# Sums of a weight block in one go, a product behind the operand splits, and two transfers asked for one pair sooner

## The chip, the cores and the metric

The kernel runs on one core of one Trainium2 chip. The metric is the device time of the whole program in microseconds (us). A core has one engine for matrix products (TensorE, PE in the profile, with its weight loads as PEld), three for elementwise work (VectorE = DVE, ScalarE = ACT, GpSimd = POOL), and a queue, SyncE (SP), which here issues all transfers between memory and the core. Each engine works through its own instructions in order and waits where an operand or a buffer is not ready.

## The reference

Two branches read the same input x of 2048 rows and 640 columns (written A_x and B_x in the inputs; x stands for A_x).

```python
xn = _layernorm(x)                                    # first branch: on the normalised rows
q, k, v = (xn @ wqkv) split into 32 heads of 20
logits  = q . k[pos - 2*w] * 20**-0.5,  w = 0..7      # a local window of 8 rows, 2 apart
attn    = softmax(logits, masked where pos - 2*w < 0)
s       = (sum over w of attn * v[pos - 2*w]) @ wo

g = x @ w_gate                                        # second branch: 640 -> 1536
u = x @ w_up
out = x + s * silu((g * u) @ w_down)                  # 1536 -> 640
```

So there are four large products (wqkv, gate and up, wo, w_down), and between the first and the third the attention, which is elementwise work on 32 heads.

## The kernel before, in words

All products are taken to the precision of float32 as three products of parts: each operand is split into a high part (`hi`, rounded for TensorE) and the remainder (`lo`). `split` (L104, L105) does it: ACT writes hi, then GpSimd writes lo. A product is hi·hi, hi·lo, lo·hi (`ALL3`).

The order of all instructions is written out by hand: each engine works in the order in which the program issues them.

1. Loading, layer norm and transpositions, to about 100 us.
2. The product with wqkv in 12 units of 8 tiles (`qkv`, L395); ACT copies each result (L401) and SP stores it (L403). Beside it runs the attention, a generator that `advance` steps on as time passes: DVE multiplies and reduces (L470, L480, L444), GpSimd adds up the output o (L447, with every second addition on DVE in the last unit), and `store_o` (L522) writes o to memory (`o_scr`). The attention is behind the products and goes on beside stage 3, until about 485 us.
3. Gate and up, one column block f = 2 to 11 after another, from about 276 to 541 us. x is taken in four chunks of 512 rows, 0 to 3. For chunks 0 and 1, `group(f)` forms seven products (L1197) of sums of weight blocks and sums of x (Strassen's scheme in Winograd's form), in the order j = 0, 5, 2, 1, 4, 3, 6. For chunks 2 and 3 the products are plain: `gate(f, 2)`, `gate(f, 3)`, `up(f, 2)`, `up(f, 3)`, each of 15 matmuls (L114).
4. The product of o with wo, by pairs of tiles p = 0 to 4 (`pair_product`, L935), and three tiles by themselves, until about 611 us; beside it the sums and splits of w_down.
5. The last products with w_down (L802) and the output, to the end.

In stage 3, the sums of the next block's weights (`w_add`, L1149) are GpSimd's: S1, S2, S3, d5, S4, written to a tile `wraw`. `w_split` splits them in two groups, S (S1 to S3) and R (S4 and d5); the gate's and up's own columns are G and U. The seven products go into three banks: A, B and C. Of chunk 1's result, `gate_b` (L1174, DVE) completes the gate and `up_b` the up half: an addition (L1177) and the product of both (L1178) on GpSimd, and then the store of h (`store_h`, L1161). Of chunk 0's, `gate_a` (L1182) and `up_a` (L1185) are DVE's. What stands in the list `unfinished` is issued by the next `finish_piece`: `up_a` in `gate(f, 2)` that follows the group, behind its 15 matmuls and the copy of their result by ACT (L1226). Between `group(f)` and `gate(f, 2)` stands `next_sums(f + 1)`. So GpSimd has, per block: S1, S2, an addition of o, S3, d5, an addition of o, the addition of `up_b`, its product, S4, the lo parts of S and R, an addition of o. ACT has the hi parts of S and R and then the copy of `gate(f, 2)`.

The first block of these, f = 2, has its sums and the splits of S and G made during stage 2: `first_parts` is a list of seven steps, of which `paced` takes 0.42 at each of the 8 tiles of a unit; what is left at the end is made at once (`step(100)`).

In stage 4, `load_pair(p)` asks for the two tiles of o of pair p in four transfers (`load_o`, L619), and `turn_pair(p)` transposes them on DVE (L625) and forms sums (L887 to L890). `hi_pair` (L910, ACT) and `lo_pair` (L914, DVE) split them. `pair_product` copies or adds a result (L938, L941, L944, L946, L949) and stores it (L947, L950). The raw tiles of pairs 1, 3 and 4 share the two buffers of the tag "t". `out_proj` does the single tiles (ACT copies L651 and L664, DVE L653), and the w_down sums are DVE's (L705, L708, L712, L715).

Of the kernel before, what the change touches and what calls it, by code (L numbers as in the profile page):

```python
# [51 lines left out]
def kernel(  # L52
# [23 lines left out]
    def st(shape, tag, bufs, dt=F32):  # L76
        cnt[0] += 1
        return sb.tile(shape, dt, tag=tag, bufs=bufs, name=f"{tag}_{cnt[0]}")
# [39 lines left out]
    def slot(shape, dt=F32R):  # L118
        return st(shape, "s", SLOTS, dt)
# [221 lines left out]
    UN = [(g, r) for g in range(len(GROUPS)) for r in range(DIL)]  # L341
# [238 lines left out]
    unfinished = []  # L580
# [34 lines left out]
    def load_o(s, n, t):  # L615


        for b in range(NQ):
            nc.sync.dma_start(t[b * QB:(b + 1) * QB].rearrange("i n (q c) -> i (n q) c", c=QC),  # L619
                              o_scr[s // NE, b, s % NE:s % NE + n].rearrange("n (q i) c -> i (n q) c", i=QB))  # L620
        for i in range(n):
            o_t[s + i] = t[:, i]
# [249 lines left out]
    def load_pair(p):  # L872
        t = slot([P, 2, D], F32) if p == 2 else st([P, 2 if p else 6, D], "t" if p else "kv", 2)
        if not p:
            wo_sum.append(t[:, 2:].rearrange("p a (b c) -> p (a b) c", c=HALF))
            t = t[:, :2]
        load_o(2 * p, 2, t)
        t = t.rearrange("p a c -> p (a c)")
        pair_raw[p] = t[:, :3 * KS * P].rearrange("p (a c) -> p a c", c=P)
# [43 lines left out]
    def pair_product(p, j):  # L923
        place = "ACACABA"[j]
        new = j in (0, 1, 5)
        if new:
            bank[p, place] = pt([P, HALF], {"A": "q", "B": "g", "C": "u"}[place], {"A": 3, "B": 2, "C": 2}[place])
        b = bank[p, place]
        runs = [(pair_in(p, H_IN[j], k, i), w_part(W_IN[j], k, l)) for i, l in ALL3 for k in range(KS)]
        if j in FIFTH:  # L930
            name, c = FIFTH[j]
            runs += [(pair_in(p, name, 0, i), wo_t["W0-W1"][:, l] if c is None else wo_s[KD - 1][l][:, c:c + HALF])
                     for i, l in ALL3]
        for r, (y, w) in enumerate(runs):
            nc.tensor.matmul(b, y, w, start=new and r == 0, stop=r == len(runs) - 1, skip_group_check=True)  # L935
        kept, (ya, yb) = pair_k[0], y_t.setdefault((p, "y"), [None, None])
        if j < 3:
            nc.scalar.activation(kept[:, j], b, AF.Copy)  # L938
        elif j == 3:
            ya = y_t[p, "y"][0] = st([P, D], "gh", 5)  # L940
            nc.vector.tensor_add(ya[:, HALF:], kept[:, 2], b)  # L941
        elif j == 4:
            yb = y_t[p, "y"][1] = st([P, D], "gh", 5)
            nc.vector.tensor_add(yb[:, HALF:], kept[:, 1], b)  # L944
        elif j == 5:
            nc.vector.tensor_add(ya[:, :HALF], kept[:, 0], b)  # L946
            nc.sync.dma_start(s_scr[2 * p], ya)  # L947
        else:
            nc.scalar.activation(yb[:, :HALF], b, AF.Copy)  # L949
            nc.sync.dma_start(s_scr[2 * p + 1], yb)  # L950
# [189 lines left out]
    def w_add(f, *names):  # L1140

        if f not in w_sum:
            w_sum[f] = st([P, 9, P], "wraw", 2)
        r, t = wf_raw[f], w_sum[f]
        v = {"A11": r[:, 0:2, 0], "A12": r[:, 2:4, 0], "A21": r[:, 0:2, 1], "A22": r[:, 2:4, 1], "g5": r[:, 4, 0],
             "u5": r[:, 4, 1], "S1": t[:, 0:2], "S2": t[:, 2:4], "S3": t[:, 4:6], "S4": t[:, 6:8], "d5": t[:, 8]}
        for name in names:
            a, b = W_SUM[name]
            nc.gpsimd.tensor_tensor(v[name], v[a], v[b], op=ALU.add if name == "S1" else ALU.subtract)  # L1149
# [14 lines left out]
    def group(f):  # L1164

        b = {"A": pt([P, CH], "g", 2), "C": pt([P, CH], "u", 2), "B": q_one}
        kept, later = {}, []

        def hold(j):
            kept[j] = st([P, CH], "gh", 5)  # L1170
            nc.scalar.activation(kept[j], b["ACACABA"[j]], AF.Copy)  # L1171

        def gate_b():
            nc.vector.tensor_add(kept[2], kept[2], b["C"])  # L1174

        def up_b():
            nc.gpsimd.tensor_add(kept[1], kept[1], kept[4])  # L1177
            nc.gpsimd.tensor_mul(kept[2], kept[2], kept[1])  # L1178
            store_h(f, 1, kept[2])

        def gate_a():
            nc.vector.tensor_add(kept[0], kept[0], b["B"])  # L1182

        def up_a():
            nc.vector.tensor_mul(kept[0], kept[0], b["A"])  # L1185
            store_h(f, 0, kept[0])

        w_split(f, "U")
        wf_raw.pop(f)
        for n, j in enumerate((0, 5, 2, 1, 4, 3, 6)):  # L1190
            y = b["ACACABA"[j]]
            runs = [(w_unit(H_IN[j], k)[i], x_in(W_IN[j], l, k)) for i, l in ALL3 for k in range(2)]
            if j in FIVE:
                name, ch = FIVE[j]
                runs += [(w_unit(name)[i], xT[ch][l][:, KD - 1, :]) for i, l in ALL3]
            for r, (w, x) in enumerate(runs):
                nc.tensor.matmul(y, w, x, start=j in (0, 1, 5) and r == 0, stop=r == len(runs) - 1,  # L1197
                                 skip_group_check=True)
            if j in (0, 1, 2, 4):
                hold(j)  # L1200
            finish_piece()
            for act in later:
                act()
            later = {5: [gate_a], 3: [gate_b, up_b]}.get(j, [])
            if j == 6:
                unfinished.append(up_a)
            if f < f1 and n in (3, 4):
                w_add(f + 1, *(("S1", "S2"), ("S3", "d5"))[n - 3])
            if n in beside:
                beside[n]()  # L1210
            advance(PACE * len(runs) * 0.184)
# [34 lines left out]
        advance(PACE * 2.8)  # L1246

    def next_sums(f):
        w_add(f, "S4")
        w_split(f, "S", "R")  # L1250
        w_sum.pop(f)
        if f < f1:
            load_wf(f + 1)
# [11 lines left out]
    paced = 0.0  # L1265
    for u in range(2, len(UN)):
        begin_unit(u)
        g, r = UN[u]
        for i in range(NE):
            if g + 1 < len(GROUPS) and (r, i) == (0, 1):  # L1270
                load_wq(g + 1, ((0, 3), (3, 5)))
            elif g + 1 < len(GROUPS) and r and i < KD:
                split_wq(g + 1, nc.gpsimd, (i, i + 1))
            if u == len(UN) - 3 and i == 6:
                load_wf(2)
            qkv(u, i)
            if i == 1:
                finish_piece()
            advance(PACE * GROUPS[g] * 0.38)
            paced += 0.42  # L1280
            while paced >= 1:
                paced -= 1
                step()
        if u == len(UN) - 3:
            steps.append(first_parts())
        elif u == len(UN) - 2:
            for k in range(2):
                last_difference(k)
# [71 lines left out]
    def wd_splits():  # L1360
        while to_split:
            k, part = to_split.pop(0)
            split_wd(k, part)
            if part and k + 2 < KH:
                load_wd(k + 2)

    pair_product(0, 0)
    for p in range(SP // 2):
        more = p + 1 < SP // 2
        if not more:  # L1370
            y1 = turn_o(SP)
        if p < 3:
            wd_sums()
        pair_product(p, 1)
        if more:
            hi_pair(p + 1, 0)
            lo_pair(p + 1, 0)
            if p == 3:
                wd_sums()
        else:  # L1380
            split_o(SP, y1)
        pair_product(p, 2)
        if not more:
            wd_splits()
            wd_sums()
        elif p < 3:
            hi_pair(p + 1, 2)
        pair_product(p, 3)
        if more:
            if p == 3:  # L1390
                hi_pair(p + 1, 2)
            lo_pair(p + 1, 2)
            hi_pair(p + 1, 1)
        pair_product(p, 4)
        wd_splits()
        if more:
            lo_pair(p + 1, 1)
        pair_product(p, 5)
        if p == 0:
            load_pair(3)  # L1400
        elif p == 1:
            load_pair(4)
            turn_pair(3)
        elif p == 2:
            load_o(SP, 3, st([P, 3, D], "t", 2))
            turn_pair(4)
        else:
            if p == 3:
                load_o(SP + 3, 3, st([P, 3, D], "t", 2))
            wd_sums()  # L1410
        if more:
            pair_product(p + 1, 0)
        else:
            out_proj(SP, 0)
            wd_splits()
        pair_product(p, 6)
# [25 lines left out]
    for m in range(n_prod):  # L1442
        n, j = divmod(m, 7)
# [65 lines left out]
```

## Time and profile before

| what | value |
|---|---|
| time, median of 3 runs | 769.35 us (766.48 to 770.05) |
| the profiled execution's own time | 765.59 us |
| its span | 763.8 us |
| mean granted TensorE clock | 0.997 |
| PE busy | 748.3 us |
| DVE busy | 601.5 us |
| GpSimd busy | 422.7 us |
| ACT busy | 276.0 us |

How to read it: the span is the stretch between the first and the last instruction of one profiled execution, and the time is a little longer. Busy times are sums over instructions. A line of a timeline gives the start in us from the span's beginning, the duration, the engine, the line of the kernel, the operation with its output and input tiles and their shapes, and in brackets how long the engine was idle before it and what released it. A group of waits gives the engine, the tile and the line that waited, what it waited for, the total in us, the number of times and the longest. The ends of matmuls are modelled, and a run of matmuls is shown as one row.

### The profile page before, as it was taken

How to read it: one execution, taken by the hardware profiler on the slowest of the kernel's cores; microseconds unless marked ns; L12 is line 12 of the kernel's file. 1: busy time of each engine (PE TensorE's matmuls, PEld its weight loads, DVE VectorE, ACT ScalarE, POOL GpSimd, SP SyncE). 2: the span in 40 equal slices, each digit the busy share in tenths (PEclk: the TensorE clock that was granted, in tenths of full speed). 3: DMA queues.
4: the chain of work that ended last, by engine and by line, in shares of the span. 5: the costliest groups of instructions: out<-in, count | busy, mean ns of one | idle time of the engine just before them, and what ended most of it. 6: DMA issues, size and time to landing. Idle time of an engine off the chain costs nothing. (4 is left out here: it accounts for less than half of the span.)

```text
span 763.8 us, 11642 instructions
## 1 busy us (share of the span) xinstructions
PE 748.3 (98%) x4342; PEld 688.4 (90%) x4342; DVE 601.5 (79%) x753; ACT 276.0 (36%) x534; POOL 422.7 (55%) x342
## 2 busy tenths in 40 slices
PE   8999999999999999999999999999999999999997
PEld 6989899999999988888888787788999999999997
DVE  7899995997796896989696967244888697777775
ACT  4334213233332232222222222234465564444442
POOL 5100256988966969799787987664648810000000
PEclk9999999999999999999999999999999999999999
DMA  9463537678458454464535331544487565555534
GB/s 326 142 189 101 159 105 204 209 198 217 157 161 240 134 177 127 116 185 125 145 105 148 90 87 29 170 109 105 132 224 212 186 251 186 187 187 186 186 104 139
DMA packets 101975, 123.02 MB, mean 161 GB/s; under 512 B 24376, under 2 KB 75956, under 8 KB 101918
## 3 DMA queue, kind: packets, MB, share of 16 engines
q1 hardware_dynamic: 101918, 122.28, 52.6%
q8 instruction: 34, 0.56, 0.3%
q14 instruction: 23, 0.19, 0.1%
HBM read 78.73 MB, written 42.81 MB: 159 GB/s over the span
## 5 line engine op out<-in xcount | busy, mean ns | idle before, releaser
L447 POOL TENSOR_TENSOR o<-o,t 128x800 f32<-128x800 f32 (+1 forms) x81 | 164.3, 2029 | 56.3 <-DVE o L444 45.8
L105 POOL TENSOR_TENSOR s<-wraw,s 128x768 fp32r<-128x768 f32 (+5 forms) x72 | 89.1, 1253 | 82.8 <-ACT s L104 72.1
L114 PE MATMUL g<-xc,s 128*128 128x512 f32 (+1 forms) x435 | 101.2, 387 | 4.0 <-DVE gh L1185 2.9
L470 DVE TENSOR_TENSOR t<-q,kv 128x1600 f32<-128x1600 f32 (+1 forms) x48 | 92.5, 1927 | 12.2 <-DMA kv<-qkv_scr 8.3
L114 PEld LDWEIGHTS g<-xc,s 128*128 128x128 f32 x435 | 80.6, 191 | 20.7 <-DVE gh L1185 3.3
L114 PE MATMUL u<-xc,s 128*128 128x512 f32 (+1 forms) x435 | 99.1, 383 | 0.0
L114 PEld LDWEIGHTS u<-xc,s 128*128 128x128 f32 x435 | 79.7, 188 | 15.7
L480 DVE TENSOR_REDUCE lg<-t 128x80 f32<-128x1600 f32 (+1 forms) x48 | 92.3, 1923 | 0.1
L444 DVE TENSOR_TENSOR t<-e,kv 128x800 f32<-128x800 f32 (+1 forms) x84 | 87.1, 1036 | 5.4 <-POOL o L447 5.3
L395 PE MATMUL q<-s,xc 128*128 128x300 f32 (+1 forms) x540 | 84.5, 307 | 1.4 <-DVE rstd L249 0.7
L395 PEld LDWEIGHTS q<-s,xc 128*128 128x128 f32 x540 | 79.4, 188 | 2.6 <-DVE rstd L249 1.0
L104 ACT ACTIVATE s<-wraw 128x640 fp32r<-128x640 f32 (+5 forms) x73 | 43.0, 601 | 93.4 <-POOL wraw L1149 55.5
L395 PE MATMUL g<-s,xc 128*128 128x300 f32 (+1 forms) x420 | 65.8, 308 | 0.0
L395 PE MATMUL u<-s,xc 128*128 128x300 f32 (+1 forms) x420 | 65.4, 307 | 0.0
L395 PEld LDWEIGHTS g<-s,xc 128*128 128x128 f32 x420 | 62.4, 188 | 0.0
L395 PEld LDWEIGHTS u<-s,xc 128*128 128x128 f32 x420 | 62.1, 188 | 0.0
L802 PE MATMUL q<-xc,s 128*128 128x320 f32 x270 | 42.0, 309 | 0.0
L802 PEld LDWEIGHTS q<-xc,s 128*128 128x128 f32 x270 | 40.2, 188 | 0.0
L1197 PE MATMUL g<-xc,s 128*128 128x512 f32 x150 | 37.5, 390 | 1.0 <-POOL s L105 1.0
L1238 DVE TENSOR_TENSOR gh<-u,gh 128x512 f32<-128x512 f32 x19 | 13.0, 686 | 30.7 <-PE u L114 30.7
L1171 ACT ACTIVATE gh<-g 128x512 f32<-128x512 f32 x30 | 18.0, 599 | 52.5 <-PE g L1197 51.7
L765 DVE TENSOR_TENSOR s<-s,s 128x768 fp32r<-128x768 f32 x29 | 27.8, 958 | 8.9 <-ACT s L761 8.8
(304 smaller groups left out, 1339.1 us busy)
## 6 DMA issues: line engine op xcount, KB each, us to landing
h_scr<-gh SPq DMA_DIRECT2D x48, 256.0 KB, 2.4
qkv_scr<-s SPq DMA_DIRECT2D x28, 300.0 KB, 3.7
wraw<-in_wgu SPq DMA_DIRECT2D x11, 640.0 KB, 4.4
t<-h_scr SPq DMA_DIRECT2D x8, 768.0 KB, 7.3
qkv_scr<-s SPq DMA_DIRECT2D x16, 360.0 KB, 3.1
kv<-qkv_scr SPq DMA_DIRECT2D x14, 400.0 KB, 5.1
s_scr<-gh SPq DMA_DIRECT2D x16, 320.0 KB, 3.5
gh<-s_scr SPq DMA_DIRECT2D x16, 320.0 KB, 4.0
```

The source lines that it names most:

```text
L104: nc.scalar.activation(hi, raw, AF.Copy)
L105: eng.tensor_sub(lo, raw, hi.bitcast(F32))
L114: nc.tensor.matmul(acc, a, b, start=first and n == 0, stop=last and n == len(runs) - 1)
L395: nc.tensor.matmul(p, xT[(r * NE + i) // TPC][a][:, k, t0:t0 + P], wq[g][b][k], start=n == 0, stop=n == len(runs) - 1, skip_group_check=ac ...
L444: nc.vector.tensor_mul(t.rearrange("p (n d) -> p n d", d=DH), e[:, :, w].unsqueeze(2).to_broadcast([P, NE * nh, DH]), v)
L447: return NE * c * cost, lambda: eng.tensor_add(y, y, t)
L470: nc.vector.tensor_mul(t, q, k)
L480: nc.vector.tensor_reduce(out=lg[:, :, j:j + 2].rearrange("p n a -> p a n"), in_=t.rearrange("p a (n d) -> p a n d", d=DH), op=ALU.add, ax ...
L765: nc.vector.tensor_sub(hT[m][:, 1], h_raw[n][name], hT[m][:, 0].bitcast(F32))
L802: nc.tensor.matmul(p, y[:, i, k], wd_t[name][k][:, l], start=new and r == 0, stop=r == len(runs) - 1, skip_group_check=True)
L1171: nc.scalar.activation(kept[j], b["ACACABA"[j]], AF.Copy)
L1197: nc.tensor.matmul(y, w, x, start=j in (0, 1, 5) and r == 0, stop=r == len(runs) - 1, skip_group_check=True)
```

## The change

There are four edits.

1. `up_b` keeps only the addition. The product and its store become a function `h_b`, which is put in `unfinished` ahead of `up_a`: it is issued behind the splits of S and R of the next block and behind the matmuls and the copy of `gate(f, 2)`.
2. S4 is made in `group` together with S3 and d5, no longer in `next_sums`. GpSimd's order per block becomes S1, S2, an addition of o, S3, d5, S4, an addition of o, the addition of `up_b`, the lo parts of S and R, the product, an addition of o.
3. In the last two units of stage 2, `paced` takes 0.8 steps at each tile instead of 0.42. GpSimd then makes the lo parts of S and of G for f = 2 between additions of o of these units.
4. `load_pair(3)` is issued ahead of `pair_product(0, 0)` instead of behind `pair_product(0, 5)`, and `load_pair(4)` in its place instead of one pair later. The transpositions stay where they are.

TensorE's, and DVE's, instructions keep their order.

```diff
         def up_b():
             nc.gpsimd.tensor_add(kept[1], kept[1], kept[4])
+
+        def h_b():
             nc.gpsimd.tensor_mul(kept[2], kept[2], kept[1])
             store_h(f, 1, kept[2])
...
             if j == 6:
-                unfinished.append(up_a)
+                unfinished.extend([h_b, up_a])
             if f < f1 and n in (3, 4):
-                w_add(f + 1, *(("S1", "S2"), ("S3", "d5"))[n - 3])
+                w_add(f + 1, *(("S1", "S2"), ("S3", "d5", "S4"))[n - 3])
...
     def next_sums(f):
-        w_add(f, "S4")
         w_split(f, "S", "R")
...
-            paced += 0.42
+            paced += 0.42 if u < len(UN) - 2 else 0.8
...
+    load_pair(3)
     pair_product(0, 0)
...
         if p == 0:
-            load_pair(3)
+            load_pair(4)
         elif p == 1:
-            load_pair(4)
             turn_pair(3)
```

## The prediction

> **What bounds the kernel now.** I read the page's busy shares first, then the groups of waits of TensorE, then the timeline around each of these waits.
>
> ```profile
> span 763.8 us, 11642 instructions
> PE 748.3 (98%) x4342; PEld 688.4 (90%) x4342; DVE 601.5 (79%) x753; ACT 276.0 (36%) x534; POOL 422.7 (55%) x342
> ```
>
> TensorE (PE) is busy for 98% of the span, and its instructions stand in the same order before and after the change. So the change can only act through the 15.5 us in which PE isn't busy, and through the clock. The groups of PE's waits (total, times, longest) tell how much of that lies where the change reaches:
>
> ```profile
> PE g L114 <- DVE gh L1185: 2.9, 1, 2.9
> ...
> PE g L114 <- ACT gh L1226: 1.1, 1, 1.1
> ...
> PE g L1197 <- POOL s L105: 1.0, 1, 1.0
> PE e L935 <- DVE gh L944: 1.0, 1, 1.0
> PE q L114 <- ACT gh L664: 0.8, 1, 0.8
> ...
> PE q L935 <- ACT o L938: 0.4, 1, 0.4
> ```
>
> These six single waits make 7.2 us, 0.9% of the time. Only one of the ten column blocks waits at `up_a` (L1185), one at the gate copy (L1226), one at the splits (L105): the repeated edit in the blocks pays once, not ten times. All sums below are against the profiled execution, 765.59 us (span 763.8 and 1.8 around it), which is 3.8 below the median of the runs, 769.35; I carry the difference over to the median. A change of 0.5%, 3.85 us, is about what a measurement of this kernel can tell from none.
>
> **The faster pace of the first parts (f=2).** The steps of `first_parts` are taken in the last two qkv units at 0.8 instead of 0.42 each, so that the sums and the splits of S and G come ahead of attention's additions on POOL. The rows are from the timeline (start, duration, engine, line), the last from the list of transfers (count, size, median us to landing):
>
> ```profile
> 251.55 1.92 POOL L447 TENSOR_TENSOR o<-o,t 128x800 f32<-128x800 f32 x1 [0.49 <-DVE t L444]
> 254.18 1.92 POOL L447 TENSOR_TENSOR o<-o,t 128x800 f32<-128x800 f32 x1 [0.71 <-DVE t L444]
> 261.60 3.90 POOL L447 TENSOR_TENSOR o<-o,t 128x800 f32<-128x800 f32 x2
> 265.46 0.74 POOL L1149 TENSOR_TENSOR wraw<-wraw,wraw 128x256 f32<-128x256 f32 x1
> 267.41 0.56 SPq L522 DMA_DIRECT2D o_scr<-o  x1
> 269.97 1.84 POOL L105 TENSOR_TENSOR s<-wraw,s 128x768 fp32r<-128x768 f32 x1 [3.04 <-ACT s L104]
> 273.09 0.99 DVE L444 TENSOR_TENSOR o<-e,kv 128x800 f32<-128x800 f32 x1 [0.31 <-DMA o_scr<-o]
> 276.10 1.55 POOL L105 TENSOR_TENSOR s<-wraw,s 128x640 fp32r<-128x640 f32 x1
> 277.70 0.73 PE L1197 MATMUL g<-xc,s 128*128 128x512 f32 x2 [1.00 <-POOL s L105]
> 279.49 2.54 POOL L105 TENSOR_TENSOR s<-wraw,s 128x384 fp32r<-128x384 f32 x2
> 283.06 0.84 PE L1197 MATMUL u<-xc,s 128*128 128x512 f32 x3
> o_scr<-o SPq DMA_DIRECT2D x4, 400.0 KB, 6.2
> ```
>
> The lo part of G (276.10) is what PE waits 1.00 for. Moved ahead of the two additions at 261.60, it is done some 14 us early: -1.0. Its price: S4 0.74, S 1.84 and G 1.55, together 4.1, now stand ahead of those additions, which ended at 265.5. POOL's idle 0.49 and 0.71 absorb 1.2, so they end near 268.4, the store of o goes from 267.4 to 268.4 and lands 6.2 later, and the DVE instruction at 273.09, which already waited 0.31 for that store, starts 1.0 later. POOL's chain behind it (two additions, then the lo parts of R and U, which ended at 279.49 and 2.54) is bound by DVE's products, no longer by G's 1.55; I estimate U's end at 282.5, half a us later than before. PE, 1.0 sooner, needs it at 282.5 (283.06 less 1.0, and two hi products of about 0.2 each ahead of the lo one): a loss of 0.1 at most. If no idle absorbs anything, the store is 2.2 later, U ends 1.2 later still, and PE stands there for it. I take **-0.9**, bounds -1.0 and +0.2, since the idle rows are there.
>
> **The product behind the splits, and S4 ahead (f=3 to 11).** Three things move: S4 from behind the product to behind d5, the product behind the lo parts of S and R, and on SP the load of the next weights ahead of the product's store. First f=7, the block that waits at the gate copy:
>
> ```profile
> 418.82 3.56 PE L114 MATMUL g<-xc,s 128*128 128x512 f32 x15
> 420.45 1.29 POOL L1178 TENSOR_TENSOR gh<-gh,gh 128x512 f32<-128x512 f32 x1 [3.48 <-DVE gh L1174]
> 421.76 0.38 SPq L1161 DMA_DIRECT2D h_scr<-gh  x1
> 422.30 0.68 DVE L1185 TENSOR_TENSOR gh<-gh,g 128x512 f32<-128x512 f32 x1
> 422.46 0.52 ACT L104 ACTIVATE s<-wraw 128x384 fp32r<-128x384 f32 x1 [5.23 <-POOL wraw L1149]
> 422.89 0.58 ACT L1226 ACTIVATE gh<-g 128x512 f32<-128x512 f32 x1
> 423.52 3.70 PE L114 MATMUL g<-xc,s 128*128 128x512 f32 x15 [1.14 <-ACT gh L1226]
> 427.32 0.60 ACT L1226 ACTIVATE gh<-g 128x512 f32<-128x512 f32 x1 [3.85 <-PE g L114]
> ```
>
> The copy at 422.89 stands on ACT behind the hi part of R, this one waits for S4, S4 stood behind the product, and that waits 3.48 for DVE. With S4 ahead, R's hi part is done long before. But the copy needs the matmuls that end at 422.38; the next one in line (427.32) started 0.10 behind its own (423.52 and 3.70). So it can start at 422.48, 0.41 sooner, and PE near 423.1; `up_a`, ended at 422.98, just permits that. **-0.4**, bounds 0 and -0.41: the wait of 1.14 cannot go, since two thirds of it are the copy itself. The later product costs nothing: it moves by the splits' 2.8 at most, so its store goes from 421.8 to about 424.6, and the buffer is asked for only by the next block's first copy, behind three more groups of 15 matmuls (3.4 each) from 423.5, after 434. If that cover were gone, it would be ACT and then PE that waits 2.8.
>
> Now f=9, the largest wait; the last line is the granted clock in four us (PE, PEld, DVE, ACT, POOL busy, then PEclk, DMA share, GB/s):
>
> ```profile
> 472.10 1.16 POOL L1149 TENSOR_TENSOR wraw<-wraw 128x256 f32<-128x256 f32 x2
> 473.23 2.26 POOL L447 TENSOR_TENSOR o<-o,t 128x960 f32<-128x960 f32 x1
> 475.52 2.20 DVE L447 TENSOR_TENSOR o<-o,t 128x960 f32<-128x960 f32 x1 [1.25 <-POOL o L447]
> 477.64 0.68 DVE L1185 TENSOR_TENSOR gh<-gh,g 128x512 f32<-128x512 f32 x1
> 478.38 5.31 PE L114 MATMUL g<-xc,s 128*128 128x512 f32 x15 [2.87 <-DVE gh L1185]
> ```
>
> ```profile
> 478.00:482.00 4.00, 3.62 (x9) 2.86 (x10) 1.39 (x2) 1.01 (x2) 4.00 (x4) 0.60 0.22 66
> ```
>
> POOL runs without a gap from S3 and d5 (472.10) into an addition of o (473.23), DVE's own addition waits for that, `up_a` stands behind it on DVE, and PE behind `up_a`. The change puts S4 (0.74) exactly between 472.10 and 473.23. Nothing in the chain is idle but what waits for it, so PE waits 3.6 instead of 2.87: **+0.7**, the one place where the edit hurts. The clock shows a second price here. The mean of 0.60 in this stretch, and 15 matmuls in 5.31 where f=7 has 3.56, say that 1.75 us were lost to a halved clock after the idle. I take that as unchanged; bounds for the place are -1.0 (slow stretch gone by its phase) and +2.5 (a second one).
>
> The Trainium skill, page "TensorE: Matmul & The Clock Gate", section "Why this matters for your kernels", advises no PE-idle gap above some 3 us. By that rule before (2.87) would pass and after (3.6) would be slowed, 1.75 dearer than my sum. The trace differs: a gap of 2.87 was already followed by the halved clock, so the measurement decides and I add nothing for it.
>
> **Pairs 3 and 4 loaded a pair sooner.**
>
> ```profile
> 560.13 2.24 SPq L619 DMA_DIRECT2D t<-o_scr  x4
> 567.57 1.57 DVE L625 STREAM_TRANSPOSE s<-t 128x640 f32<-128x640 f32 x2 [1.64 <-DMA t<-o_scr]
> 574.61 1.14 PE L935 MATMUL e<-xc,xc 128*128 128x320 f32 x6 [0.95 <-DVE gh L944]
> 579.64 1.14 PE L935 MATMUL q<-xc,xc 128*128 128x320 f32 x6 [0.37 <-ACT o L938]
> 580.03 1.24 POOL L105 TENSOR_TENSOR xc<-wraw,xc 128x320 fp32r<-128x320 f32 x1 [2.63 <-ACT xc L104]
> 595.67 4.66 PE L114 MATMUL q<-s,s 128*128 128x320 f32 x30 [0.80 <-ACT gh L664]
> ```
>
> Pair 4's four transfers, issued from 560.13, are waited for 1.64 by the transposition at 567.57. DVE is behind from there: PE waits 0.95 for its addition L944 and 0.37 for a copy that stands behind the next transposition's result. Issued a pair sooner, behind the split of pair 1's operands, the four land in time; DVE gains up to 1.64, which is more than 0.95 and 0.37 together, so both go: -1.3. What is late next is POOL's row of w_down splits, which starts at 580.03 behind ACT and ends in the wait at 595.67. Its start hangs on the same DVE chain, so it moves along; if it doesn't (its raw weights come by DMA), the 1.3 is given back there. The queue SP gets four transfers of pair 3 behind the last store of h, where it has nothing else to issue until pair 0's first result is stored, and four of pair 4 ahead of a store whose buffer is one of five and is asked for a pair later: 0. I take **-1.3**, bounds 0 and -1.64.
>
> **Sum:** -0.9 - 0.4 + 0.7 - 1.3 = -1.9. The profiled execution would go from 765.6 to 763.7, the median from 769.35 to about 767.5.
>
> **Rivals.**
> *All bounds fall well.* -1.0 - 0.4 - 1.0 - 1.64 = -4.0, so 765.3. For it: the slow stretch hangs on where the idle falls. Against: the idle grows.
> *S4 costs in every block (slower).* In f=3 to 9 S4 also stands ahead of an addition of o, for which DVE waits, and `up_a` is queued on DVE. Where `up_a` has less than 0.74 to spare, each such block loses it: seven of them, f=9 counted already, 6 x 0.74 = +4.4, so 771.9. It decides where POOL has no gap ahead of DVE's next read. Against: POOL was idle 3.48 in f=7, and no block but f=9 shows a wait for `up_a`; for it: `up_a` in f=7 has only 0.1 left once the copy is early.
> *The tail doesn't move.* Splits of w_down end when they did, the 1.3 returns as a longer wait at 595.67: -0.6, so 768.8. POOL's 15 us without a gap before that wait speak for it.
> *Clock.* The 3.6 us of idle brings a second slow stretch: +1.75 on the sum, 769.2.
>
> **How the numbers follow.** Forecast 0.56, all well 0.14, S4 everywhere 0.10, tail unmoved 0.14, clock 0.06. The ends of all parts give -4.0 to +2.7, 765.3 to 772.1; the three runs of before lie 2.9 below and 0.7 above their median, which I add at each end: 762.5 to 772.5. Faster than 765.5 are most of the second case and, by the spread of the runs, a seventh of the first: 0.20. Slower than 773.2 is the upper part of the S4 case, with blocks that lose more than S4's own length, and what I have not seen: 0.12. The rest, 0.68, is within 0.5%.
>
> **What would show it.** Right: no wait of PE for L105 near 277; the wait at the gate copy of f=7 near 0.7; f=9's wait at 3.6, with S4 between d5 and the addition of o, and one slow stretch behind it; no wait for o_scr at the transposition of pair 4, and none for L944. Wrong: a wait for `up_a` in other blocks, a wait at U's lo part near 282, a wait at 595 that grew by as much as the tail gained, or a change in the clock elsewhere.

## The result and the profile after

| | before | changed |
|---|---|---|
| median of the runs, us | 769.35 (766.48 to 770.13, 7 runs) | 763.9 (762.35 to 766.17, 7 runs) |
| the profiled execution's own time, us | 765.59 | 763.91 |
| its span, us | 763.8 | 762.1 |
| PE busy, us | 748.3 | 750.4 |

The ratio of the times is 0.9935, with a 95% interval of 0.9916 to 0.9953: the changed kernel is faster by 5.0 us (3.6 to 6.5). On another occasion, with 12 runs of the changed kernel, it was 0.9955 (0.9932 to 0.9977). The forecast was 1.9 us faster.

The two profiled executions differ by only 1.7 us, and PE is busier after the change by 2.1 us, though it does the same work. The groups of PE's waits of the changed kernel (line numbers behind 1177 are 2 higher than before) show why this pair of executions must not be subtracted as it stands:

```profile
PE g L114 <- DVE gh L1187: 2.5, 1, 2.5
...
PE g L114 <- ACT gh L1228: 0.7, 1, 0.7
...
PE q L114 <- ACT gh L664: 0.5, 1, 0.5
```

Of the six waits quoted in the prediction, three are gone (L105 at f = 2, L944 and L938 in stage 4) and three are shorter. That alone is over 3 us. What hid it is the rate of the qkv products, in the timeline of PE (start, duration, line), first before the change, then after:

```profile
270.84 2.56 PE L395 MATMUL q<-s,xc 128*128 128x360 f32 x15
273.24 2.56 PE L395 MATMUL g<-s,xc 128*128 128x360 f32 x15
```

```profile
272.54 2.63 PE L395 MATMUL u<-s,xc 128*128 128x360 f32 x15
275.01 2.63 PE L395 MATMUL q<-s,xc 128*128 128x360 f32 x15
```

From start to start, 15 matmuls took 2.40 us in the execution before and 2.47 in that after: 160.0 and 164.4 ns for one. In the execution after, stage 2 ran at the slower rate from 131 us on, behind a stop of 0.56 us at that place. Together this makes 4.3 us by the stage's end, at a granted clock of 1.00 in both. The experiments show that this belongs to the execution and not to the kernel.

To compare kernels without it, I take from the traces the time between the starts of two given PE instructions, which are the same in all kernels since PE's order is. The stretches: f = 2 (from PE's first product of the block over 14 matmuls), f = 7 (40 matmuls around the gate copy), f = 9 (31 around the wait for `up_a`), pair products (75 matmuls, with the waits for L944 and L938), and the last products with wo (100, with the wait for L664). "Halved clock" means that the trace records a granted clock of 0.5 for the 3.4 us behind that wait.

| execution | f = 2 | f = 7 | f = 9 | halved clock at f = 9 | pair products | last products with wo |
|---|---|---|---|---|---|---|
| before | 4.27 | 10.51 | 11.82 | yes | 12.85 | 16.04 |
| before, second (e1) | 4.16 | 10.51 | 10.23 | no | 13.17 | 16.04 |
| before, third (e11) | 4.52 | 10.51 | 11.83 | yes | 12.80 | 16.03 |
| changed | 3.04 | 10.05 | 9.77 | no | 11.00 | 15.79 |
| changed, second (e9) | 2.97 | 10.05 | 9.77 | no | 11.00 | 15.79 |

By the means of these rows the change brings -1.3 at f = 2, -0.46 at f = 7, -0.46 at f = 9 without the clock (10.23 to 9.77), -1.9 in the pair products and -0.25 behind them: -4.4 us. The halved clock at f = 9 adds 1.6 (11.82 less 10.23) to some executions. All other stretches between PE's instructions agree within 0.15 us in these five, the qkv stage and the first 130 us aside.

### The profile page after: what moved, and what is told of

Read it like the earlier page. It is cut to its first block, busy times and chain, and to the rows that moved or that the text cites. A ratio compares the mean times of both kernels' runs of the same rounds, so it can differ in the third digit from the quotient of the medians.

```text
span 762.1 us, 11644 instructions
## 1 busy us (share of the span) xinstructions
PE 750.4 (98%) x4342; PEld 691.3 (91%) x4342; DVE 598.4 (79%) x753; ACT 276.5 (36%) x534; POOL 421.9 (55%) x342
## 5 line engine op out<-in xcount | busy, mean ns | idle before, releaser
L105 POOL TENSOR_TENSOR s<-wraw,s 128x768 fp32r<-128x768 f32 (+5 forms) x72 | 89.0, 1250 | 80.6 <-ACT s L104 70.8
L114 PE MATMUL g<-xc,s 128*128 128x512 f32 (+1 forms) x435 | 99.6, 383 | 3.1 <-DVE gh L1187 2.5
L1228 ACT ACTIVATE gh<-g 128x512 f32<-128x512 f32 x20 | 12.0, 599 | 68.6 <-PE g L114 63.0
L1171 ACT ACTIVATE gh<-g 128x512 f32<-128x512 f32 x30 | 18.0, 599 | 51.4 <-PE g L1199 46.8
```

What stands on the lines that cost most here:

```text
L105: eng.tensor_sub(lo, raw, hi.bitcast(F32))
L114: nc.tensor.matmul(acc, a, b, start=first and n == 0, stop=last and n == len(runs) - 1)
```

## The experiments

Every kernel was timed beside the kernel before on the same chip; ratios are against it.

**e1, e11: the kernel before, twice more; e9: the changed kernel once more.** No edit.

> The kernel before, unchanged, profiled once more. Theory A: the first profiled execution of it (765.59 us) was a rare fast one. The usual one runs the matmuls of the qkv stage (L395) from 131 us on at 164.4 ns each instead of 160.0 (as the profiled execution of the changed kernel does), which is +4.3 us by 279 us; the time is then about 769.5, and since PE comes later to f=9 while attention does not, the wait at f=9 is shorter than 2.87. Theory B: the rate of L395 depends on the kernel (places of buffers, order on the other engines); this profile then shows 160.0 ns again, and the measured 5 us is a real difference against a fast stage, with more than 9 us gained elsewhere. Ratio to the kernel before 1.000 by both.

> The kernel before, one look more. Theory A: where its profile shows 164.4 ns in the qkv stage, the state belongs to the execution, since its two earlier profiles showed 160.0. The waits at f=9 (2.9), f=7 (1.1), at the tail (0.7 to 1.3 and 0.4) are there again by every theory.

> The changed kernel, unchanged, once more. Theory A (the rate of the qkv matmuls is a state of the execution, not of the kernel): its profile can show 160.0 ns where the first showed 164.4; if it does, the state is settled; if it shows 164.4 again, nothing is. Ratio against before 0.993 to 0.996: the waits that went make 4.3 us by segments of the traces, and a halved clock at f=9 that comes in some executions of both kernels.

Ratios 1.0004 (0.9978 to 1.003) for e1 and 0.9955 (0.9932 to 0.9977) for e9. The second profile of before has 160.0 ns again, the third 164.4, and the second profile of the changed kernel 160.0. PE's timeline in the last two:

```profile
270.43 2.63 PE L395 MATMUL u<-s,xc 128*128 128x360 f32 x15
272.90 2.63 PE L395 MATMUL q<-s,xc 128*128 128x360 f32 x15
```

```profile
268.24 2.56 PE L395 MATMUL u<-s,xc 128*128 128x360 f32 x15
270.64 2.56 PE L395 MATMUL q<-s,xc 128*128 128x360 f32 x15
```

The first fence is e11, the kernel before at 2.47 us for 15; the second e9, the changed kernel at 2.40. So both kernels show both rates, and Theory B is out. What Theory A says of 160.0 being rare is out as well: of the thirteen profiled executions of all kernels, seven had it at the end of the stage. The rate moves a single execution by up to 4.3 us, nearly the size of the whole gain.

The traces show where the slower rate begins. Each of the six executions that ended the stage at 164.4 ns lost 0.06 to 0.56 us at the products of 131 us, from start to start, and none of the seven others lost anything there. First the execution before, then that after the change:

```profile
131.18 2.21 PE L395 MATMUL q<-s,xc 128*128 128x300 f32 x15
```

```profile
131.60 2.37 PE L395 MATMUL q<-s,xc 128*128 128x300 f32 x15 [0.29 <-ACT s L401]
```

Three of the six (the changed kernel's first, e2 and e4) ran slower from there on; the three others (e5, e8 and e11) did so from about 198 us, where the products go from 300 to 360 columns. Whether the stop sets the rate, and by what means, stays open.

The same executions show the halved clock coming and going with the same kernel and the same wait. e1, the kernel before, waited 2.88 at f = 9 and then ran at full rate, where the first execution needed 5.31 for the same 15 matmuls:

```profile
478.22 3.72 PE L114 MATMUL g<-xc,s 128*128 128x512 f32 x15 [2.88 <-DVE gh L1185]
```

```profile
478.00:482.00 4.00, 3.78 (x16) 3.11 (x17) 1.23 (x2) 1.01 (x2) 4.00 (x4) 1.00 0.22 66
```

**e2: the pair loads alone.**

```diff
+    load_pair(3)
     pair_product(0, 0)
...
         if p == 0:
-            load_pair(3)
+            load_pair(4)
         elif p == 1:
-            load_pair(4)
             turn_pair(3)
```

> The kernel before with only the loads of pairs 3 and 4 a pair sooner. By the prediction's term: -1.3 us, ratio 0.998, no wait of the transposition of pair 4 for o_scr, none of PE at 574 and 579 us. By the two profiles (PE gains 1.25 at 574, 0.63 at 579 and 0.36 at 595): -2.2, ratio 0.997. If the w_down splits swallow it: 1.000 and a longer wait at 595.

Ratio 0.9977 (0.9951 to 1.0002). Of its waits, those for L944 and L938 are gone and the one for L664 is 0.5:

```profile
PE g L114 <- DVE gh L1185: 2.9, 1, 2.9
...
PE g L114 <- ACT gh L1226: 1.1, 1, 1.1
...
PE q L114 <- ACT gh L664: 0.5, 1, 0.5
```

The pair products take 11.00 and the last products with wo 15.79, exactly as in the changed kernel: -1.9 and -0.25 against the mean of before, all of it from this edit. The 1.3 of the prediction were too little.

**e3: the faster pace alone.**

```diff
-            paced += 0.42
+            paced += 0.42 if u < len(UN) - 2 else 0.8
```

> The kernel before with only the faster pace of the first parts. By the prediction's term: -0.9 us, ratio 0.999, no wait for the lo part of G at f=2. By the rival that this stage also moves attention against PE and so the wait at f=9: -0.9 and a change of the f=9 wait by a us or more, and with it the halved clock comes or goes (1.75).

Ratio 0.9976 (0.995 to 1.0003). The stretch at f = 2 falls to 2.97. The wait at f = 9 is 3.2 here against 2.9. DVE's wait for the store of o one block earlier, on which it hangs (e7, below), is longer by as much, 2.39 against 2.05; in e11, with no edit, it is 2.23. Together with the block edits the pace leaves the wait at 2.5, as these have it alone (e4, below). That the pace costs something at f = 9 is so not shown, and the rival's "a us or more" isn't borne out.

**e4: the two edits in the blocks, without pace and pair loads; e5: S4 alone; e6: the product alone.** e5 has the two S4 hunks of the change, e6 the two of `h_b`, e4 all four.

> The kernel before with only the two edits in the blocks (S4 ahead, the product behind the splits). By the prediction's terms: -0.4 at f=7 and +0.7 at f=9, together +0.3 us, ratio 1.000, the wait at f=9 0.7 longer than that of the kernel before in the same state of the qkv stage. By the rival that the blocks gain beyond these two places: -1 to -3 us, ratio 0.996 to 0.999, and the wait at f=9 no longer than before.

> The kernel before with S4 alone moved ahead. Theory C: the wait at f=9 fell in the changed kernel because the product behind the splits lets the splits end 1.3 us sooner, so the next weights (640 KB) are loaded sooner and lie less in the way of the store of o at f=8, for which DVE waits 2.05 us before and 0.98 with both block edits; S4 itself costs its 0.73 as predicted. Then here DVE's wait for that store stays at 2.05 and PE's wait at f=9 grows from 2.9 to 3.6; the copy's wait at f=7 falls from 1.1 to 0.7; time against before about +0.3 us, ratio 1.000. Rival D: S4 ahead shortens the wait itself (the chain was ended by something else): the wait at f=9 is 2.5.

> The kernel before with the product alone behind the splits; S4 stays behind the additions. Theory C: DVE's wait for the store of o at f=8 falls from 2.05 to about 1.0, and PE's wait at f=9 from 2.9 to about 1.8, that is 0.7 less than in the changed kernel; the copy's wait at f=7 falls to 0.7 here too, since S4 no longer stands behind the product; about -1.5 us, and -3 where the halved clock stays away (it has to when no clock window is idle for most of its length), ratio 0.996 to 0.998. Rival D: the wait at f=9 stays at 2.9.

The ratios are 0.9986 (0.9959 to 1.0014) for e4, 0.9995 (0.9968 to 1.0022) for e5 and 0.9946 (0.9922 to 0.997) for e6. The waits at f = 9 and f = 7, in this order of kernels:

```profile
PE g L114 <- DVE gh L1187: 2.5, 1, 2.5
...
PE g L114 <- ACT gh L1228: 0.7, 1, 0.7
```

```profile
PE g L114 <- DVE gh L1185: 3.7, 1, 3.7
...
PE g L114 <- ACT gh L1226: 0.7, 1, 0.7
```

```profile
PE g L114 <- DVE gh L1187: 2.2, 1, 2.2
...
PE g L114 <- ACT gh L1228: 0.7, 1, 0.7
```

Either edit by itself brings the copy's wait at f = 7 to 0.7. At f = 9 they work against each other: S4 alone lengthens the wait from 2.9 to 3.7, the product alone shortens it to 2.2, both give 2.5. Why the product reaches f = 9 at all is to be seen on SP and DVE one block earlier. First before the change, then after it (SP's issues, and DVE's first product of the next unit of attention, which overwrites o):

```profile
451.99 0.35 SPq L163 DMA_DIRECT2D wraw<-in_wgu  x1
452.43 0.39 SPq L1161 DMA_DIRECT2D h_scr<-gh  x1
454.20 0.99 SPq L522 DMA_DIRECT2D o_scr<-o  x2
...
459.72 1.16 DVE L444 TENSOR_TENSOR o<-e,kv 128x960 f32<-128x960 f32 x1 [2.05 <-DMA o_scr<-o]
```

```profile
453.09 0.35 SPq L163 DMA_DIRECT2D wraw<-in_wgu  x1
454.33 0.91 SPq L1161 DMA_DIRECT2D h_scr<-gh  x2
456.54 0.99 SPq L522 DMA_DIRECT2D o_scr<-o  x2
...
461.07 1.16 DVE L444 TENSOR_TENSOR o<-e,kv 128x960 f32<-128x960 f32 x1 [0.93 <-DMA o_scr<-o]
```

The 640 KB of the next weights go into the buffer that the splits have just read. With the product behind the splits these end one product (1.3) sooner, and the load is issued 3.45 ahead of the store of o instead of 2.21. The store then lands 4.5 us behind its issue instead of 5.5, and DVE, which may not overwrite o before, waits 0.93 instead of 2.05. All additions of the last unit, and with them `up_a` at f = 9, come that much sooner. e6 falls short of its expectation, 2.2 and not 1.8: its load is as far ahead of the store (3.46), but DVE still waits 1.41, so how far ahead the load is doesn't settle the landing alone. In time e6 gained more than expected, 4.1 us (2.3 to 6.0). Its waits at f = 7 and f = 9 account for 1.1 of that and the clock for about 1 (the mean granted clock of its timed runs is 0.9983, that of the kernel before 0.9969); the runs don't show where the rest comes from.

**e7: the weight load of block 10 behind the store of o.**

```diff
     def next_sums(f):
...
-        if f < f1:
+        if f < f1 and f != f0 - 1:
             load_wf(f + 1)
...
         up(f, 2, g2)
+        if f == f0 - 2:
+            load_wf(f0)
         up(f, 3, g3)
```

> The kernel before with the weight load of block 10 issued behind the store of o at f=8 instead of ahead of it; nothing else moves. Theory C: the store lands sooner than the 5.5 us that it takes beside the load, DVE's wait of 2.05 falls by 1 to 2, and PE's wait at f=9 from 2.9 by as much, to 0.9 to 1.9; then no halved clock behind it; ratio 0.995 to 0.998. Rival: the store's landing does not depend on the load (its own 5.5 us are its length); the waits stay at 2.05 and 2.9, ratio 1.000.

Ratio 0.9963 (0.9938 to 0.9988). SP and DVE at f = 8, and PE at f = 9:

```profile
453.77 0.99 SPq L522 DMA_DIRECT2D o_scr<-o  x2
454.85 0.78 SPq L163 DMA_DIRECT2D wraw<-in_wgu  x1
```

```profile
457.71 1.16 DVE L444 TENSOR_TENSOR o<-e,kv 128x960 f32<-128x960 f32 x1 [0.46 <-DMA o_scr<-o]
```

```profile
476.38 3.70 PE L114 MATMUL g<-xc,s 128*128 128x512 f32 x15 [1.30 <-DVE gh L1185]
```

With no load ahead of it, the store is through 3.9 us behind its issue (453.77 to 457.71). DVE's wait falls from 2.05 to 0.46, and PE's at f = 9 from 2.87 to 1.30, by the same 1.6. This moves one transfer in the queue and nothing else, so the chain from the weight load over the store to `up_a` is shown, and the rival is out.

**e8: pace, pair loads, product behind the splits and the late load, S4 in its old place; e10: the same with S4 ahead.** e10 is the changed kernel with the edit of e7, e8 is that without the two S4 hunks.

> The changed kernel with S4 back behind the product's old place and with the late weight load of block 10: pair loads, pace, product behind the splits. If the parts add up: f=2 -1.1, f=7 -0.4, f=9's wait at 0.8 to 1.8 and no halved clock, tail -2.1; against before -5 to -7 us, ratio 0.991 to 0.994, and 1 to 2 us below the changed kernel. If DVE is held by something else at f=8 the wait at f=9 stays at 2.5 and it equals the changed kernel.

> The changed kernel with the weight load of block 10 behind the store of o; it is the earlier combination of all but S4, with S4 ahead. Theory C: PE's wait at f=9 is that combination's 1.4 plus S4's 0.73, 2.1, where the changed kernel has 2.5; the rest as there. Ratio against before about 0.993, 0.5 to 1 us above the combination without S4. If S4 costs nothing there: 1.4.

The ratios are 0.9908 (0.9876 to 0.994) for e8, median 761.12 us, and 0.9913 (0.9882 to 0.9945) for e10, median 761.25. The wait at f = 9 is 1.4 in e8 and 2.0 in e10, so S4 costs 0.6 there:

```profile
PE g L114 <- DVE gh L1187: 1.4, 1, 1.4
```

```profile
PE g L114 <- DVE gh L1187: 2.0, 1, 2.0
```

Both have lower ratios than the changed kernel, though the intervals overlap with its own; e10 ran beside e9, 761.25 against 763.99. Their own difference, 0.6 us in the trace, is too small for these runs. The version that I would keep is e8.

The chain can be read in all thirteen profiled executions at once. PE's idle time at f = 9, from the start that was due to the actual one, is DVE's wait for the store of o at f = 8 and some 0.97 more, and S4's own 0.73 where S4 stands ahead:

| execution | DVE's wait for the store at f = 8 | S4 ahead | PE's idle at f = 9 | idle less that wait, and less 0.73 for S4 |
|---|---|---|---|---|
| before | 2.05 | no | 3.03 | 0.98 |
| e11, before again | 2.23 | no | 3.19 | 0.96 |
| e3 | 2.39 | no | 3.35 | 0.96 |
| e6 | 1.41 | no | 2.41 | 1.00 |
| e7 | 0.46 | no | 1.46 | 1.00 |
| e5 | 2.23 | yes | 3.89 | 0.93 |
| changed | 0.93 | yes | 2.61 | 0.95 |
| e10 | 0.49 | yes | 2.18 | 0.96 |

The other five lie between 0.94 and 1.00.

## Why the prediction was right or wrong

The direction and the range (762.5 to 772.5) held; the size did not, and the likeliest outcome of the forecast, within 0.5% of before with 0.68, did not come: the measured 0.65% belongs to the case "faster", which had 0.20. (By the prediction's own addition the range would end at 762.4 and 772.8; nothing hangs on it.) Term by term, with the price by start to start:

- **The faster pace, -0.9 predicted: right in mechanism, -1.3 measured** (4.32 as the mean of three to 3.00). The wait for the lo part of G went, and U's lo part cost nothing: no execution with this edit waits for it at f = 2 (the single wait of 0.2 for a lo part of U in e9 is at 334 us, in f = 4, and e7, without this edit, has the same). The term was under-sized because a PE wait costs more than its row shows (below). The first execution's 1.0 was also one value of a wait that goes from 0.5 to 1.2 in others: over all eight executions without this edit (e2 and e4 to e7 too) the stretch has a mean of 4.1, so 1.1 is the better figure for the gain.
- **f = 7, -0.4 predicted: right, -0.46**, just past its bound of -0.41. The copy now starts at the end of its own matmuls, the wait of 1.1 keeps 0.7, and either edit alone is enough for it. By its row the copy (0.58) was half of the 1.14, not the two thirds that the prediction says; the rest of what stayed is the way to it and from it.
- **f = 9, +0.7 predicted: wrong in sign, -0.46.** The step that failed is "Nothing in the chain is idle but what waits for it", by which I let the chain of additions start where it did before. S4's own price was right: e5 has 0.8 more, e10 0.6 more than e8. But the chain begins a block earlier, at DVE's wait of 2.05 for the store of o. I had counted the later product's store and buffer and not that the splits, and with them the buffer and the load of the next weights, come sooner by the product's length. I wrote that the load moves ahead of the product's store on SP and gave it no price. It was worth 1.1, and the table behind e10 shows the chain holding in every execution.
- **The pair loads, -1.3 predicted: right in mechanism, -2.2 measured** (e2). Both waits went. The splits of w_down moved along, as I had taken it: in e2 GpSimd's row of them began 2.1 sooner against the products ahead of this stage, PE was 1.85 sooner, and the wait at 595 shrank by the 0.25 between. The rest is again the price of a wait: the two shown as 0.95 and 0.37 make 1.32, the stretch lost 1.85.
- **The clock, taken as unchanged.** 1.75 was nearly the right price for the halved stretch (1.6 by the segments), but it isn't a fixed cost of the kernel: before had it in two of three profiled executions, the changed kernel in none of two, though e4, with the same wait of 2.5, had it. The mean granted clocks of the timed runs say more. The two executions of before that had it show 0.997 and 0.996, the one without it 1.000; of 82 timed runs of before 63 show 0.997 or less and the others 0.999 or more, while of 19 of the changed kernel 6 show 0.996 or less and the others 0.998 or more. The means, 0.9969 and 0.9978, differ by about 0.7 us of such a run, and that much I would put down to the clock. With the shorter waits of e7, e8 and e10 the halved clock did not come at f = 9 in the profiled executions, and all 16 timed runs of e7 and e8 show 0.999 or more.

Sum by the traces: -4.2 to -4.4, and some -0.7 for the clock, against -5.0 (-3.6 to -6.5) measured, and -3.5 (-1.8 to -5.2) on the other occasion. The rival "all bounds fall well" came out nearest in time, though not in its reason; its bounds of -1.0 at f = 2 and -1.64 at the tail were passed. "S4 costs in every block" is out: e5 pays at f = 9 alone, and no other block waits for `up_a`. "The tail doesn't move" is out by e2. "Clock" had its condition, an idle time above 3.6, in e5 alone (3.89), and one window was halved there, not two.

The rows of one profiled execution against another would have led astray: they gave 1.7, close to the forecast's 1.9, out of a gain of 4.4 in waits, 1.6 from the clock and a loss of 4.3 in the qkv stage.

**Why a PE wait costs more than its row.** Matmul ends are modelled. In the first execution of before, the six matmuls ahead of the wait shown as 0.95 began at 572.62; at 146.7 ns each the next was due at 573.50 and began at 574.61, which is 1.11. The six behind it then lasted 1.14 instead of 1.04. So 0.95 cost 1.2, and 0.37 cost 0.6 by the same reckoning (due at 579.11, begun at 579.64, and 0.1 behind it).

## What to carry to other kernels

When a step is moved on one engine, follow not only who waits for that step but what all the others that come sooner set free: a buffer that is read sooner starts its next load sooner, and that load can collide less, or more, with a store on which another engine waits. Compare kernels stretch by stretch between the same PE instructions, since the spans of two single executions can differ by more than the change. Where a wait of PE is removed, count it from start to start and not by the idle time shown.

## What the runs showed of the hardware

**The clock window.** The trace's records of the granted clock put all changes within an execution on a grid of 3.413 us, with its own phase in each. I split PE's idle time at f = 9 over the two grid windows that it touches:

| execution | idle, start to start | the larger share in one window | halved clock behind it |
|---|---|---|---|
| before | 3.03 | 2.98 | yes |
| e1, before again | 3.05 | 1.62 | no |
| e2 | 3.03 | 1.96 | yes |
| e4 | 2.67 | 2.13 | yes |
| e5 | 3.89 | 2.21 | yes |
| changed | 2.61 | 1.48 | no |
| e9, changed again | 2.61 | 2.08 | no |
| e6 | 2.41 | 1.77 | no |
| e8 | 1.55 | 1.53 | no |

Of the others, e3 (2.58) and e11 (2.99) had the halved clock, e7 (1.46) and e10 (1.35) not. At f = 9, where a window was idle for 2.13 us or more, the next one was granted half the clock; at 1.77 or less it never was; between, at 1.96 and 2.08, it went both ways. So the same wait costs 1.6 us more or not by its phase, and no wait below 1.8 us there was followed by the halved clock. These limits are not shown to hold elsewhere: in the first 10 us of e5 and e10 a window was halved behind one of which the profile shows only 1.4 and 1.2 us idle, and in e4, with 1.2, none was. The Trainium skill, page "TensorE: Matmul & The Clock Gate", part 1, gives the same window, 3413 ns and free-running, and the trace agrees. Its section "Why this matters for your kernels" advises no idle gap above some 3 us; here the measurement differs, since in e4 a gap of 2.67 was followed by the halved clock. (The gap of 2.87 that the prediction names is 3.03 from start to start, so it settles less.)

**The rate of the qkv matmuls.** 160.0 or 164.4 ns for 360 columns at a granted clock of 1.00, constant over tens of us. Executions that became slower at 131 us lost 3.8 to 4.3 us by the end of the stage, those that became slower at 198 us (e5, e8 and e11) 2.2 to 2.5. Behind the first dozen matmuls of f = 2 (0.07 us of that stretch) no stage showed two rates.

**A store beside a load.** The same store of o (128x960 f32, 480 KB) took 5.5, 4.5 and 3.9 us from issue until DVE could go on, with the 640 KB load issued 2.2 ahead of it (before), 3.5 ahead (changed), and behind it (e7). Over all executions these are 5.5 to 5.9 (six), 4.5 to 5.0 (four, with 5.0 in e6) and 3.9 to 4.1 (three).
